# First batch's scores and value products as single float32 products, in a block-sparse attention and MLP kernel

## The chip, the cores and the metric

The kernel runs on one core of a Trainium2 chip. A core has a matrix engine (TensorE: PE for products, PEld for weight loads), VectorE (DVE), ScalarE (ACT), GpSimd (POOL) and SyncE (SP), which here issues nearly all DMAs. Each engine takes its instructions in the order in which the program lists them; engines wait for each other by semaphores. The metric is the time of one execution on the device, in microseconds (us), lower is better.

## The reference

Attention over 4 batches, 8 heads, 768 positions and 64 dimensions, with a mask in blocks of 32 positions, followed by an MLP with 512 inputs, 2048 inner and 512 outer columns on 3072 rows; `scale` is 1/8, `window` 1, and every block of queries has 3 sampled blocks of keys:

```python
scores = scale * np.matmul(q, k.transpose(0, 1, 3, 2))
mask = np.abs(blk_i - blk_j) <= window
mask = mask | (blk_i == 0) | (blk_j == 0) | (blk_i == n_blocks - 1) | (blk_j == n_blocks - 1)
for qb in range(n_blocks):
    for kb in sampled_blocks[qb]:
        mask[qb * block:(qb + 1) * block, kb * block:(kb + 1) * block] = True
scores = np.where(mask, scores, -1000000000.0)
scores = scores - np.max(scores, axis=-1, keepdims=True)
attn = np.exp(scores)
attn = attn / (np.sum(attn, axis=-1, keepdims=True) + 1e-09)
attn_out = np.matmul(attn, v)
...
x = np.ascontiguousarray(attn_out.transpose(0, 2, 1, 3)).reshape(B * S, H * D)
h = x @ w_in
sp = np.where(h > 20.0, h, np.log1p(np.exp(np.minimum(h, 20.0))))
g = h * np.tanh(sp)
y = g @ w_out
```

## The kernel before, in words

**Numbers.** A product of float32 data is made of fp16 parts: every operand is scaled by a power of two, rounded to a high part, and the rest kept as a low part. Three products stand for one: high x high, low x high, high x low (`PROD`, L659). The scale comes from the data: products of a tile with itself (`gram_k`, `gram_q`, `gram_v`, L373), their diagonal summed (L388), a sum over partitions by a float32 product with ones (`tp_k` and others, L396), and an integer root (`root`, L405 to L409). `parts` writes the high part on ScalarE (L500) and the low part on VectorE (L504); some tiles of q are done on ScalarE and GpSimd in its place (`APART`, L518 to L535).

**Attention.** Each batch is 13 jobs: two dense ones (first and last block of queries, against all 768 keys) and 11 pairs of query blocks. A query block of a pair sees 8 blocks of 32 keys: three neighbours (read from `kt`, 96 columns), the two ends and three sampled ones (copied to `kg` by GpSimd L611 or ScalarE L608, 160 columns). The blocks' numbers are read from memory into registers of the engine that copies, or of SP (L580), which gathers the value blocks (`vg`) from a copy of v in DRAM (`vd`, written at L553; gathered at L628 to L635).
`scores` (L664) runs on tiles of 64x32 of the array: four pairs of heads by two heads, eight places. Then come the maxima (L732 to L737, VectorE), the exponentials (L756, ScalarE), transposes of the probabilities (`t`, L680, TensorE), and their high part `ph` (L779, ScalarE). The low part `pl` is made on VectorE (L783), or, in jobs 0 to 5 of all 52 (`i < APL`), by a correcting product on TensorE (L787) and another pass of ScalarE (L792). The value products (`o_fn`, L818) use four tiles of 128x32: three products for each of the four pairs of head parity and key half, so 48 a transposed piece. A column of ones beside v gives the sum; L837 to L841 divide by it, and transposes (`tx`) give x.

**MLP.** w_in and w_out arrive as 8-byte numbers; pieces are loaded (L893, three buffers `wr`) and decoded on VectorE by three integer operations each (L901, L904, L907), which run through the first 175 us beside the attention of the first batch. Products with w_in are `h_None` (L1068), those with w_out `y` (L1162). `fill` (L1506) puts products without use where TensorE would be idle.

**Order.** All this is written as tasks (`add(engine, cost, function, ...)`) and a list of task numbers, `ORDER`, gives the sequence in which they are emitted; the engines' programs follow from it. The first batch stands at the start: k, q and v are loaded (`load`, L432), scaled and split, and the first w_in pieces follow.

Of the kernel before, what the change touches and what calls it, by code (L numbers as in the profile page):

```python
# [9 lines left out]
F32 = mybir.dt.float32  # L10
# [11 lines left out]
PSC = 4096.0  # L22
# [3 lines left out]
RINGS = dict(s=1, t=2, o=1, h=2, y=1, raw=6, wr=3, pt=2, ph=4, pl=4, xh=3, xl=3, mx=3, nb=3, r=2,  # L26
# [193 lines left out]
def attn_mish_kernel(ctx: ExitStack, tc: tile.TileContext, qT, kT, v, sampled, blocks, w_in, w_out, out):  # L220
# [38 lines left out]
    vd = [dram.tile([S + BS, H, VW], F16, name=f"vd{b}") for b in range(B)]  # L259
# [18 lines left out]
    osc = const.tile([P, B], F32, name="osc")  # L278

# [10 lines left out]
    def which(new):  # L290
# [38 lines left out]
        z = room.bitcast(F16)[0:BS, 0:H * VW]  # L329
        nc.gpsimd.memset(z, 0.0)  # L330
        for b in range(B):
            nc.scalar.dma_start(out=vd[b][S:S + BS].rearrange("s h d -> s (h d)"), in_=z)
# [23 lines left out]
    vgs = [at_.tile([P, 2, H, VW], F16, name=f"vg{n}", tag=f"vg{n}", bufs=1) for n in range(NVG)]  # L356
    RAW = H * VW
# [59 lines left out]
    def load(b, what, js, ring="raw", after=()):  # L417

        keys = [("raw", what, b, j) for j in js]
# [15 lines left out]
        add("SP", 0.5 * n, fn, r=after, w=keys,  # L435
            new=[(ring, key) for key in keys], key=-5 if b == 0 else 0, lat=3.6 if b else 3.0,
# [19 lines left out]
    def scales(b, what, j, cls):  # L456
# [4 lines left out]
        def fn():  # L461
# [4 lines left out]
            root(kp, sc, iv, SQ if b else 0)  # L466
            if q:
# [10 lines left out]
    def parts(b, what, j, cls):  # L478
# [34 lines left out]
        kh = ("hi",) + key  # L513
        if (what, b, j) in APART:
# [35 lines left out]
    APART = {("q", 0, 1), ("q", 0, 2), ("k", 1, 0), ("k", 1, 1), ("k", 1, 2)}  # L550
# [9 lines left out]
    def globals_(b):  # L560

        def fn(n):
            kb = tl["kt", b].rearrange("p r (j k) -> p r j k", k=BS)[:, :, 0:NB:NB - 1]
            nc.gpsimd.tensor_copy(out=kgs[n][:, :, WK + BS:WK + 3 * BS].rearrange("p r (j k) -> p r j k", k=BS), in_=kb)
# [3 lines left out]
    def globals_v(b, n):  # L568
        def fn():
            for s, j in enumerate((0, NB - 1)):  # L570
                nc.sync.dma_start(out=vgs[n][s * BS:(s + 1) * BS, 1], in_=vd[b][j * BS:(j + 1) * BS])
# [27 lines left out]
    def gather_k(su):  # L599
# [3 lines left out]
        def fn(eng):  # L603
            for k, c0 in slots(su):
                dst = kgs[n][:, :, c0:c0 + BS]
# [8 lines left out]
        if su["whole"]:  # L614
            add("DVE", 0.5, lambda: nc.vector.tensor_copy(
                out=kgs[n][:, :, 0:WK], in_=tl["kt", b][:, :, (qb - 1) * BS:(qb + 2) * BS]),
                r=KT3(b), w=[("kw", n)], use=[("kt", b)], key=-2, port=True)

    def gather_v(su):
# [6 lines left out]
        def fn():  # L626
            vg = vgs[n]
# [11 lines left out]
    def fetch_dense(su):  # L639
# [4 lines left out]
        def fn(j):  # L644
            if j < NVG:
                vt = vgs[j]
            else:
                vt = new(sb, "raw", ("vt", b), [P, RAW]).bitcast(F16).rearrange("p (c h d) -> p c h d", h=H, d=VW)
# [15 lines left out]
    def scores(su, s, c0, pieces, first, last):  # L664
# [4 lines left out]
        for n, (a, c) in enumerate(PROD):  # L669
            for m, (cs, src, ks) in enumerate(pieces):  # L670
                for i in range(NPR):
                    for g in range(2):
# [4 lines left out]
                            stop=last and n == len(PROD) - 1 and m == len(pieces) - 1)  # L677
# [20 lines left out]
    def attend(job):  # L698

        b, i, sus, nt, dense = job["b"], job["i"], job["sus"], job["nt"], job["dense"]  # L700
        nsu = len(sus)
# [6 lines left out]
        def s_fn():  # L708
# [7 lines left out]
            else:  # L716
                for w, su in enumerate(sus):
                    qb = su["qb"]
                    kg = kgs[su["ng"] % NKG]
# [23 lines left out]
        def nb_fn():  # L743
            mx, nb = tl[kmx], new(sb, "nb", ("nb", i), [P, 2, 2])
            for w in wq:
                nc.scalar.activation(out=nb[:, :, w], in_=mx[:, :, w], func=AF.Copy,
                                     scale=tl["ns", b, sus[w.start]["qb"] // TB][:, 1:2])
        add("ACT", 0.28 * len(wq), nb_fn, r=[kmx] + [("ns", b, t) for t in qts], w=[("nb", i)],
            new=[("nb", ("nb", i))], key=-1.5)

        def ex_fn(n):
            if n == 0:
# [4 lines left out]
                out=o, in_=x, func=AF.Exp, bias=nb[:, g, w:w + 1], scale=tl["ns", b, sus[w]["qb"] // TB][:, 0:1])  # L757
# [7 lines left out]
        for n in range(2):  # L765
            add("ACT", 1.7 if dense and n == 0 else 1.15, lambda n=n: ex_fn(n),
                r=[kmx, ("nb", i), ks] + (k2 if dense else []) + [("ns", b, t) for t in qts],
# [10 lines left out]
        def ph_fn(j):  # L778
            nc.scalar.activation(out=new(at_, "ph", ("ph", i, j), [P, 2, 2, P], F16), in_=tl["t", i, j], func=AF.Copy,  # L779
                                 scale=PSC)  # L780
# [931 lines left out]
```

## Time and profile before

| | |
|---|---|
| Three runs | 736.14, 738.39, 739.52 us; median 738.39 |
| Profiled execution: span | 735.3 us, 3.1 below the median |
| TensorE busy (PE) | 695.8 us, 95% |
| VectorE busy | 581.1 us, 79% |
| ScalarE busy | 585.3 us, 80% |
| GpSimd busy | 286.9 us, 39% |
| DMA | 103.61 MB, mean 141 GB/s |

The span is the time between the first and the last record of one execution; the runs' times have a little around it. The busy shares are means over 735 us: in the first 120 us no engine is busy throughout, later TensorE is. The views used below are windows (busy time of each engine in a stretch), the chain that ended last, followed back from the end to what released each step, timelines (one line an instruction or a run of like ones), and groups of like instructions by form.

### The profile page before, as it was taken

To read this page: it belongs to the slowest core of one execution; us is meant where nothing else is said; L and a number is where in the kernel's file an instruction comes from. 1 tells how busy PE (TensorE), PEld (TensorE's weight loads), DVE (VectorE), ACT (ScalarE), POOL (GpSimd) and SP (SyncE) were. 2 spreads that over 40 slices of the span, in tenths; PEclk is the share of its full clock that TensorE was granted. 3 is DMA by queue.
4 is the path that set the end of the run, shared out by engine and by line. 5 is a ranking of instruction groups with operands and counts; after the bars stand their busy time and mean duration, and the time that the engine had idled before them with its cause. 6 is when DMAs were issued, how large, how long until landed. Compare 5 with 4: busy or idle time off the path is not lost.

```text
span 735.3 us, 28986 instructions
## 1 busy us (share of the span) xinstructions
PE 695.8 (95%) x11839; PEld 539.4 (73%) x11839; DVE 581.1 (79%) x1167; ACT 585.3 (80%) x929; POOL 286.9 (39%) x390
## 2 busy tenths in 40 slices
PE   5656889999999999999999999999999999999997
PEld 4445668875767777777677677676768888888886
DVE  6988889897788878798688798899887683656565
ACT  3685769999889998988778897987988786777772
POOL 2021423526453451545551546586732103020241
PEclk9987899999999999999999999999999999999999
DMA  9887785741555564444533644564356300000101
GB/s 328 287 221 223 231 245 153 237 146 53 171 153 152 156 203 140 139 148 125 176 105 104 202 145 153 155 174 134 110 168 201 134 29 1 30 1 1 44 6 54
DMA packets 60042, 103.61 MB, mean 141 GB/s; under 512 B 8579, under 2 KB 20868, under 8 KB 59908
## 3 DMA queue, kind: packets, MB, share of 16 engines
q1 hardware_dynamic: 58992, 98.86, 43.5%
q10 hardware_dynamic: 916, 2.89, 1.3%
q8 instruction: 93, 1.52, 0.9%
q14 instruction: 41, 0.34, 0.1%
HBM read 84.58 MB, written 17.14 MB: 138 GB/s over the span
## 4 chain that ended last, share of the span: by engine, by line
PE 86%; DMA 5%; DVE 4%; SPq 2%; ACT 1%; issue 1%; DVEq 0%
PE h_None L1068 33%; PE y L1162 19%; PE yr L1281 11%; PE t L680 6%; PE obank L818 6%; PE s L674 5%; DMA vg<-vd 2%; PE obank L1281 2%; PE tx L680 2%; DMA wr<-in_moe_w_in_dram 1%; DMA wor<-in_moe_w_out_dram 1%; DMA raw_k<-in_k_dram 1%; SPq L580 1%; SPq L635 1%; DVE v L504 1%
## 5 line engine op out<-in xcount | busy, mean ns | idle before, releaser
L1068 PEld LDWEIGHTS <-wi 128*128 128x128 f16 x2304 | 223.4, 98 | 33.7 <-issue 1.5
L1068 PE MATMUL h_None<-xh,wi 128*128 128x256 f16 x1152 | 205.7, 273 | 0.2
L611 POOL COPY kg<-kt 128x256 f16 x246 | 110.2, 481 | 153.5 <-PE s L674 127.2
L1068 PE MATMUL h_None<-xl,wi 128*128 128x256 f16 x576 | 157.0, 273 | 0.0
L1162 PE MATMUL y<-wo,g 128*128 128x512 f16 x588 | 140.3, 379 | 0.0
L1162 PEld LDWEIGHTS <-g 128*128 128x128 f16 x672 | 64.3, 99 | 61.3 <-issue 1.3
L756 ACT ACTIVATE pt<-s,nb,ns 128x256 f32<-128x256 f32 (+1 forms) x208 | 107.7, 585 | 1.5 <-DVE wo L907 0.7
L1120 POOL TENSOR_TENSOR g<-hs_None,g 128x1024 f16<-128x1024 f32 x32 | 73.7, 2302 | 63.3 <-DVE g L1116 41.6
L779 ACT ACTIVATE ph<-t 128x512 f16<-128x512 f32 x112 | 65.6, 596 | 25.6 <-PE t L680 24.1
L783 DVE SCALAR_TENSOR_TENSOR pl<-t,ph 128x512 f16<-128x512 f32 x99 | 67.0, 684 | 23.1 <-ACT ph L779 23.0
L1079 ACT ACTIVATE hs_None<-h_None,gsc 128x512 f32<-128x512 f32 x96 | 65.6, 691 | 24.3 <-PE h_None L1068 19.5
L1107 DVE SCALAR_TENSOR_TENSOR hs_None<-us_None,hs_None 128x1024 f32<-128x1024 f32 x48 | 62.0, 1292 | 21.6 <-ACT us_None L1106 21.6
L680 PE MATMUL t<-ident,pt 128*128 128x128 f32 x448 | 69.2, 287 | 7.9 <-ACT pt L756 4.7
L1068 PE MATMUL h_None<-xr,wi 128*128 128x256 f16 x576 | 67.9, 273 | 0.0
L680 PEld LDWEIGHTS t<-ident,pt 128*128 128x128 f32 x448 | 54.1, 148 | 18.7 <-issue 4.8
L737 DVE TENSOR_REDUCE mx<-s 128x4 f32<-128x1024 f32 x44 | 53.6, 1218 | 10.2 <-PE s L674 10.2
L1098 ACT ACTIVATE us_None<-hs_None,hsc 128x1024 f32<-128x1024 f32 x48 | 54.9, 1146 | 4.4 <-DVE sg L1148 1.6
L818 PEld LDWEIGHTS <-ph 128*32 128x32 f16 x2408 | 43.3, 97 | 17.1 <-issue 9.6
L818 PE MATMUL obank<-vg,ph 128*32 128x129 f16 (+2 forms) x2168 | 46.6, 211 | 6.0 <-DMA vg<-vd 5.2
L1105 ACT ACTIVATE us_None<-us_None 128x1024 f32<-128x1024 f32 x48 | 50.8, 1060 | 1.1 <-POOL us_None L1103 0.7
L1106 ACT ACTIVATE us_None<-us_None 128x1024 f32<-128x1024 f32 x48 | 50.7, 1060 | 0.4
L1281 PEld LDWEIGHTS <-sg 128*128 128x128 f16 x480 | 47.0, 98 | 5.4
(263 smaller groups left out, 1274.2 us busy)
## 6 DMA issues: line engine op xcount, KB each, us to landing
vg<-vd SPq DMA_DIRECT2D x320, 65.0 KB, 2.4
vg<-vd SPq DMA_DIRECT2D x80, 195.0 KB, 3.1
wr<-in_moe_w_in_dram SPq DMA_DIRECT2D x8, 1024.0 KB, 8.6
vd<-v SPq DMA_DIRECT2D x12, 520.0 KB, 3.4
vg<-vd SPq DMA_DIRECT2D x12, 520.0 KB, 5.0
raw_k<-in_k_dram SPq DMA_DIRECT2D x12, 512.0 KB, 5.3
raw_q<-in_q_dram SPq DMA_DIRECT2D x12, 512.0 KB, 6.0
raw_v<-in_v_dram SPq DMA_DIRECT2D x12, 512.0 KB, 5.7
```

Of the source, the lines that this page charges most:

```text
L611: nc.gpsimd.tensor_copy(out=dst, in_=tl["kt", b][:, :, ds(j, BS)])
L680: nc.tensor.matmul(out, src, ident, start=start, stop=stop, is_transpose=True)
L756: ex = lambda o, x, g, w: nc.scalar.activation(out=o, in_=x, func=AF.Exp, bias=nb[:, g, w:w + 1], scale=tl["ns", b, sus[w]["qb"] // TB][:, ...
L779: nc.scalar.activation(out=new(at_, "ph", ("ph", i, j), [P, 2, 2, P], F16), in_=tl["t", i, j], func=AF.Copy, scale=PSC)
L783: nc.vector.scalar_tensor_tensor(out=new(at_, "pl", ("pl", i, j), [P, 2, 2, P], F16), in0=tl["t", i, j], scalar=PSC, in1=tl["ph", i, j], o ...
L818: nc.tensor.matmul(obank[cs, at:at + v1 - v0], p[:, k, g, cs], vt[:, k, 2 * c + g, v0:v1], start=j == 0 and g == 0 and k == 0 and n == 0, ...
L1068: nc.tensor.matmul(h[:, f2, 0:n].rearrange("p (s q) -> p s q", q=BS), wi[:, fp, w, cc, fs], x[:, s0:s0 + sn, cc], start=f2 == 0 and k == 0 ...
L1079: nc.scalar.activation(out=tl[kq][:, 2 * (fp % 2):2 * (fp % 2) + 2, 0:n], in_=tl[kh][:, :, 0:n], func=AF.Copy, scale=gsc[:, fp:fp + 1])
L1107: add("DVE", 1.32 * c, lambda: nc.vector.scalar_tensor_tensor(out=hs(), in0=us(), scalar=-0.5, in1=hs(), op0=ALU.add, op1=ALU.mult), r=[ku ...
L1120: add("POOL", 2.3 * c, lambda: nc.gpsimd.tensor_tensor(out=g(1), in0=hs(), in1=g(0), op=ALU.subtract), r=[kq, ("gh",) + kp], w=[kp], use=[kg],
L1162: nc.tensor.matmul(tl[ky], tl["g", b, t, k][:, g, f, q], wo_at(fc)[:, w], start=fc == 0 and n == 0, stop=fc == NFC - 1 and n == 2)
L1281: nc.tensor.matmul(R(i), lhs, rhs, start=head and j == n == 0, stop=k == NFC // 4 - 1 and j == 1 and n == 2, skip_group_check=True)
```

## The change

For batch 0 (`PLAIN = (0,)`) keys, queries and values stay float32:

- k and q are loaded straight into `kt` and `q`, so the products for their scales, the roots and both parts go, and with them the scale in the exponentials, which becomes the constant 1/8.
- v is copied by ScalarE (`v<-raw_v`, 65 float32 a head with the ones column, as many bytes as 130 fp16), stored and gathered as before. v's scale is still worked out, since the MLP's scales use it; it enters as `ivr` when the sums are divided.
- Scores are one float32 product for each of the eight places and pieces in place of three. The value products are one for each of the places in place of three, 16 a piece in place of 48. No low parts of the probabilities are made; `ph` is float32, and one ring holds for the other batches what `ph` and `pl` held.
- `ORDER` keeps its sequence with the dropped tasks taken out, but the loads of k and q of batch 0 stand later: behind v, two or three pieces of w_in and register loads of SP.

The core of the diff:

```diff
+    PLAIN = (0,)
+    vd = [dram.tile([S + BS, H, D + 1], F32, name=f"vd{b}") if b in PLAIN else
+          dram.tile([S + BS, H, VW], F16, name=f"vd{b}") for b in range(B)]
...
+    kfs = [x.rearrange("p r k -> p (r k)").bitcast(F32).rearrange("p (r k) -> p r k", r=NPR) for x in kgs]
+    kgv = lambda b, n: (kfs if b in PLAIN else kgs)[n]
...
     def load(b, what, js, ring="raw", after=()):
...
             for j, key in zip(js, keys):
+                if b in PLAIN and what != "v":
+                    dst = new(at_, "kt", ("kt", b), [P, NPR, S]) if what == "k" and j == 0 else \
+                        tl["kt", b] if what == "k" else new(at_, "q", key, [P, NPR, TT])
+                    nc.sync.dma_start(
+                        out=dst[:, :, j * TT:(j + 1) * TT] if what == "k" else dst,
+                        in_=(kT if what == "k" else qT)[b, :, :, j * TT:(j + 1) * TT].rearrange("r d s -> d r s"))
+                    continue
...
+        if b in PLAIN:
+            add("ACT", 1.16, lambda: copy("ACT"), r=[kr, ("ends",) + key], w=[key, ("done",) + key], use=[key], key=cls,
+                also=[("DVE", 0.75, lambda: copy("DVE"), True)])
+            return
...
-        for n, (a, c) in enumerate(PROD):
+        prods = ((0, 0),) if b in PLAIN else PROD
+        for n, (a, c) in enumerate(prods):
             for m, (cs, src, ks) in enumerate(pieces):
                 for i in range(NPR):
                     for g in range(2):
...
+            if plain:
+                continue
             if i < APL:
                 add("PE", 0.23, lambda j=j: td_fn(j), r=[("ph", i, j)], w=[kj], key=-3, lat=0.25, kind=("T", i))
...
                 prods = ((hi, 0, 2 * D + 1), (lo, 0, D + 1)) if whole else ((hi, 0, D + 1), (hi, D + 1, 2 * D + 1), (lo, 0, D + 1))
+                if plain:
+                    prods = ((hi, 0, D + 1),)
                 for n, (p, v0, v1) in enumerate(prods):
...
-    for j in T3:
-        sums(0, "k", j, AT0)
-    scales(0, "k", 0, AT0)
-    sums(0, "q", 0, AT0)
-    scales(0, "q", 0, AT0)
-    for j in T3:
-        parts(0, "k", j, AT0)
-    parts(0, "q", 0, AT0)
```

`ORDER` itself is a table of numbers, 117 lines of it replaced. What it and the code do is seen at three places. Names: `raw_k`, `raw_q`, `raw_v` are loaded tiles, `kt` all keys of the batch, `wr` a loaded piece of w_in, `offv` the table of value offsets, `s` scores, `mx` maxima; numbers behind a name tell copies apart, and line numbers of the changed file are some 35 to 50 higher there.

SP, from its start, before:

```order
L432 DMA raw_k_0_159<-in_k_dram 128x4x256
L432 DMA raw_k_1_161<-in_k_dram 128x4x256
L432 DMA raw_k_2_163<-in_k_dram 128x4x256
L432 DMA raw_q_0_165<-in_q_dram 128x4x256
L432 DMA raw_v_0_179<-in_v_dram 128x2x512
L432 DMA raw_v_2_181<-in_v_dram 128x2x512
L432 DMA raw_v_1_191<-in_v_dram 128x2x512
L580 TENSOR_LOAD offv
...
L893 DMA wr_227<-in_moe_w_in_dram 128x4x512
L893 DMA wr_240<-in_moe_w_in_dram 128x4x512
```

and in the changed kernel:

```order
L448 DMA raw_v_0_160<-in_v_dram 128x2x512
L448 DMA raw_v_2_162<-in_v_dram 128x2x512
L448 DMA raw_v_1_164<-in_v_dram 128x2x512
L616 TENSOR_LOAD offv
...
L949 DMA wr_184<-in_moe_w_in_dram 128x4x512
L949 DMA wr_186<-in_moe_w_in_dram 128x4x512
...
L435 DMA kt_206<-in_k_dram 128x4x256
...
L949 DMA wr_245<-in_moe_w_in_dram 128x4x512
L435 DMA kt_206<-in_k_dram 128x4x256
...
L435 DMA kt_206<-in_k_dram 128x4x256
...
L435 DMA q_0_293<-in_q_dram 128x4x256
```

The keys and the query tile have moved from the head of the queue behind v, two loads of `offv` into registers, three pieces of w_in and more such loads.

VectorE, from the maxima of the first dense scores on, before:

```order
L732 TENSOR_REDUCE mx_514<-s_387 128x2
L734 TENSOR_REDUCE mx_514<-s_0_0_412 128x1
L734 TENSOR_REDUCE mx_514<-s_0_1_413 128x1
L735 TENSOR_TENSOR mx_514<-mx_514 128x2
L504 SCALAR_TENSOR_TENSOR v_0_473<-raw_v_0_179,sc_v_0_469,v_0_473 128x16x64
L904 SCALAR_TENSOR_TENSOR wi<-wr_227,wi 128x1024
L907 SCALAR_TENSOR_TENSOR wi<-wr_227,wi 128x1024
L504 SCALAR_TENSOR_TENSOR v_1_476<-raw_v_1_191,sc_v_0_469,v_1_476 128x16x64
L901 TENSOR_SCALAR wi<-wr_240 128x1024
L504 SCALAR_TENSOR_TENSOR v_2_479<-raw_v_2_181,sc_v_0_469,v_2_479 128x16x64
L901 TENSOR_SCALAR wi<-wr_312 128x1024
```

and in the changed kernel, from the last step of v's scale on:

```order
L416 TENSOR_SCALAR sc_v_0_369<-tp_v_0_316 128x1
L486 TENSOR_SCALAR ivr<-iv_x 128x1
L771 TENSOR_REDUCE mx_410<-s_319 128x2
L773 TENSOR_REDUCE mx_410<-s_0_0_328 128x1
L773 TENSOR_REDUCE mx_410<-s_0_1_329 128x1
L774 TENSOR_TENSOR mx_410<-mx_410 128x2
L960 SCALAR_TENSOR_TENSOR wi<-wr_184,wi 128x1024
L963 SCALAR_TENSOR_TENSOR wi<-wr_184,wi 128x1024
L957 TENSOR_SCALAR wi<-wr_186 128x1024
L957 TENSOR_SCALAR wi<-wr_245 128x1024
```

The three low parts of v (L504) have gone from between the decoding steps; the maxima stand where they stood, ahead of decoding the first piece of w_in.

TensorE, at the first dense scores and the first pair's scores, before:

```order
L396 MATMUL tp_v_0_384<-ss_v_0_382,ones 128x1
L674 LDWEIGHTS q_0_315
L674 MATMUL s_387<-kt_238,q_0_315 32x512
L674 LDWEIGHTS q_0_315
L674 MATMUL s_387<-kt_238,q_0_315 32x512
...
L674 LDWEIGHTS q_0_315
L674 MATMUL s_604<-kt_238,q_0_315 32x96
L674 LDWEIGHTS q_0_315
L674 MATMUL s_604<-kt_238,q_0_315 32x96
```

and in the changed kernel, where a float32 product loads its own weights and is one row:

```order
L403 MATMUL tp_v_0_316<-ss_v_0_314,ones 128x1
L712 MATMUL s_319<-kt_206,q_0_293 32x512 x8
L712 MATMUL s_0_0_328<-kt_206,q_0_293 32x256
L712 MATMUL s_0_1_329<-kt_206,q_0_293 32x256
...
L712 MATMUL s_497<-kt_206,q_0_293 32x96 x8
L712 MATMUL s_497<-kg_117,q_0_293 32x160 x8
L712 MATMUL s_497<-kt_206,q_0_293 32x96 x8
L712 MATMUL s_497<-kg_118,q_0_293 32x160 x8
```

The places and their sequence are the same; each score that was three pairs of rows is one row.

## Rows read from the trace of the kernel before

**Rows 1.** Windows of 20 us: stretch, length, each engine's busy us (instructions), PEclk, DMA share, GB/s.

```profile
20.00:40.00 20.00, 11.96 (x329) 8.93 (x314) 19.21 (x31) 13.62 (x27) 0.00 (x0) 1.00 0.87 265
40.00:60.00 20.00, 12.41 (x340) 9.10 (x337) 18.44 (x36) 15.78 (x32) 6.49 (x7) 0.77 0.85 260
60.00:80.00 20.00, 15.31 (x489) 11.78 (x491) 16.20 (x41) 11.56 (x23) 2.10 (x6) 0.72 0.66 184
...
140.00:160.00 20.00, 20.00 (x341) 16.27 (x340) 18.45 (x47) 20.00 (x34) 9.49 (x10) 1.00 0.49 155
```

**Rows 2.** Chain of waits, 0 to 125 us: start us, us, what.

```profile
1.80 6.08 DMA raw_k<-in_k_dram
...
31.78 9.24 DMA wr<-in_moe_w_in_dram
...
84.35 0.94 ACT q L529
...
86.44 3.93 PE h_None L1068 x36
...
114.19 0.49 PE obank L818 x47
```

**Rows 3.** TensorE's timeline, 7 to 20 us: start us, us, line, operation, tiles, shape, count.

```profile
7.93 1.03 PE L373 MATMUL gram_k<-raw_k 128*128 128x128 bf16 x8 [0.54 <-DMA raw_k<-in_k_dram]
9.51 0.56 PE L396 MATMUL tp_k<-ss_k,ones 128*128 128x1 f32 x2 [0.54 <-DVE gram_k L388]
...
18.44 2.12 PE L674 MATMUL s<-kt,q 64*32 64x512 f16 x48
```

**Rows 4.** TensorE's timeline, 200 to 216 us: float32 transposes at full clock.

```profile
204.94 0.27 PE L680 MATMUL tx<-ident,xs 128*128 128x128 f32 x1
...
214.69 1.09 PE L680 MATMUL t<-ident,pt 128*128 128x128 f32 x8
```

**Rows 5.** TensorE's timeline, 113 to 115 us: value products of one piece.

```profile
114.12 0.24 PE L818 MATMUL obank<-vg,ph 128*32 128x65 f16 x8
114.19 0.20 PE L818 MATMUL obank<-vg,pl 128*32 128x65 f16 x4
114.22 0.24 PE L818 MATMUL obank<-vg,ph 128*32 128x65 f16 x8
```

**Rows 6.** Window of L674 alone, 110 to 120 us: PE, PEld, PEclk, DMA share, GB/s.

```profile
110.00:120.00 10.00, 1.00 (x96) 0.85 (x96) 1.00 0.44 126
```

**Rows 7.** Groups by form, 86 to 175 us: shapes, count, busy us, mean ns, idle before.

```profile
L783 DVE SCALAR_TENSOR_TENSOR pl<-t,ph 128x512 f16<-128x512 f32 x15 | 10.0, 684 | 1.7 <-ACT ph L779 1.7
...
L818 PE MATMUL obank<-vg,pl 128*32 128x65 f16 x244 | 7.2, 193 | 0.0
...
L674 PE MATMUL s<-kg,q 64*32 64x160 f16 x192 | 4.0, 234 | 0.0
...
L674 PE MATMUL s<-kg,q 64*32 64x256 f16 x48 | 0.8, 271 | 0.0
L674 PE MATMUL s<-kt,q 64*32 64x512 f16 x24 | 0.8, 379 | 0.0
```

**Rows 8.** Window from 86 to 120 us, columns as in the first group.

```profile
86.00:120.00 34.00, 30.63 (x798) 26.00 (x796) 29.05 (x47) 25.73 (x44) 11.90 (x22) 1.00 0.73 208
```

**Rows 9.** SP's timeline, 0 to 20 us: the loads' issue.

```profile
4.83 3.44 SPq L432 DMA_DIRECT2D raw_v<-in_v_dram  x3
```

**Rows 10.** VectorE's timeline, 0 to 22 us.

```profile
8.57 0.18 DVE L327 TENSOR_SCALAR offv<-z 1x72 int32<-1x72 f32 x1
...
21.99 1.29 DVE L504 SCALAR_TENSOR_TENSOR v<-raw_v,sc_v,v 128x1024 f16<-128x1024 f32 x1
```

**Rows 11.** Window from 15 to 20 us, columns as in the first group.

```profile
15.00:20.00 5.00, 2.89 (x50) 1.80 (x56) 3.95 (x9) 2.24 (x4) 4.98 (x11) 1.00 1.05 387
```

**Rows 12.** Groups by form, 0 to 86 us: what the low parts of probabilities take.

```profile
L792 ACT ACTIVATE pl<-t 128x512 f16<-128x512 f32 x11 | 6.5, 599 | 3.8 <-PE t L787 3.8
...
L787 PE MATMUL t<-ph,neg 128*128 128x512 f16 x12 | 5.4, 480 | 1.7 <-ACT ph L779 1.7
```

More of the change, by code (lines that the diff above doesn't have):

```diff
@@ L278, in attn_mish_kernel @@
     osc = const.tile([P, B], F32, name="osc")
+    ivr = const.tile([P, 1], F32, name="ivr")
     ctx.enter_context(tc.manual_schedule())
@@ L417, in load @@
     def load(b, what, js, ring="raw", after=()):
-        keys = [("raw", what, b, j) for j in js]
+        plain = b in PLAIN and what != "v"
+        keys = [(what if plain else "raw", *((b, j) if plain else (what, b, j))) for j in js]
+        kt = ("kt", b)
         def fn():
             for j, key in zip(js, keys):
+                if b in PLAIN and what != "v":
[5 more added lines that the diff above has]
+                    continue
                 raw = new(sb, ring, key, [P, RAW]) if ring == "raw" else \
@@ L434, in load @@
         n = len(js)
-        add("SP", 0.5 * n, fn, r=after, w=keys,
-            new=[(ring, key) for key in keys], key=-5 if b == 0 else 0, lat=3.6 if b else 3.0,
+        if plain:
+            ring = "kt" if what == "k" else "q"
+        add("SP", 0.5 * n, fn, r=after, w=keys, use=[kt] if plain and what == "k" and js[0] else (),
+            new=[(ring, kt if plain and what == "k" else key) for key in keys if not (plain and what == "k" and key[-1])], key=-5 if b == 0 else 0, lat=3.6 if b else 3.0,
             kind=("dma", 1.6 * n, n))
@@ L676, in scores @@
                             src[gs, a * NPR + i, ks], start=first and n == 0 and m == 0,
-                            stop=last and n == len(PROD) - 1 and m == len(pieces) - 1)
+                            stop=last and n == len(prods) - 1 and m == len(pieces) - 1)
     def transpose(out, src, start, stop):
@@ L747, in nb_fn @@
                                      scale=tl["ns", b, sus[w.start]["qb"] // TB][:, 1:2])
-        add("ACT", 0.28 * len(wq), nb_fn, r=[kmx] + [("ns", b, t) for t in qts], w=[("nb", i)],
+        add("ACT", 0.28 * len(wq), nb_fn, r=[kmx] + [("ns", b, t) for t in qts if not plain], w=[("nb", i)],
             new=[("nb", ("nb", i))], key=-1.5)
@@ L766, in attend @@
             add("ACT", 1.7 if dense and n == 0 else 1.15, lambda n=n: ex_fn(n),
-                r=[kmx, ("nb", i), ks] + (k2 if dense else []) + [("ns", b, t) for t in qts],
+                r=[kmx, ("nb", i), ks] + (k2 if dense else []) + [("ns", b, t) for t in qts if not plain],
                 w=[("p", i, n)], new=[("pt", k) for k in kps] if n == 0 else (), use=kps, key=-1.5)
@@ L809, in o_fn @@
                 tl[ko] = obank
-            w, apart = 0 if dense else j, i >= SPLIT
-            vt = vgs[sus[w]["ng"] % NVG] if not dense else tl["vt", b, j] if sus[0]["qb"] else tl["v", b, j]
-            hi, lo = tl["ph", i, j], tl["pl", i, j]
+            w, apart = 0 if dense else j, i >= SPLIT and not plain
+            vt = vgv(b, sus[w]["ng"] % NVG) if not dense else tl["vt", b, j] if sus[0]["qb"] else tl["v", b, j]
+            hi, lo = tl["ph", i, j], tl.get(("pl", i, j))
             for g, k in ((g, k) for g in range(2) for k in range(2)):
@@ L1376, in attn_mish_kernel @@
         load(0, "k", [j])
-    load(0, "q", [0], "hs")
+    load(0, "q", [0])
     for j in T3:
```

295 lines of the change are left out of this document (162 added, 133 removed), and 18 rows, old and new, of the table ORDER.

## The prediction

> **What bounds the kernel now.** I read the windows of 20 us first, then the chain of waits, then the timelines of TensorE, SP and VectorE. The windows [rows 1] show two regimes. From 140 us on TensorE is busy all the time, so whatever its work grows by there is added to the time. Before 80 us it is not: it is busy 11.96, 12.41 and 15.31 us of three stretches of 20, and in the first two VectorE is the fullest engine with 19.21 and 18.44. The chain of waits [rows 2] says what this first stretch waits for: the keys, which land at 7.88 us (1.80 + 6.08), and at 31.78 us a piece of w_in, which was fetched only when VectorE had decoded an earlier one and given back its buffer. At 86.44 us the first MLP products start, and soon afterwards TensorE is full. All of the change lies in the first 175 us. So there are two questions: by how much does the first MLP product come later, and how much TensorE work is added behind it.
>
> **What a float32 product costs.** Everything rests on this. The trace has float32 products on the whole array only. tp_k is one product in the program and two matmuls in the trace [rows 3]: a float32 product is two streams, one behind the other, on the same place of the array. For the rate of a stream I take the float32 transposes: eight of 128 columns take 1.09 us, and one alone is recorded with 0.27, so they start (1.09 - 0.27)/7 = 117 ns apart, about 2 cycles of 2.4 GHz a column [rows 4]. A half is then 2 cycles a column, a product 4. That the halves run at fp16's single cycle is the lower end of the price.
>
> The Trainium skill (FP8 and Floating Point Precision, TensorE Precision Notes) counts four passes through the array for a true float32 product. By that rule the lower end falls away and the sum below stands; no row here has such a product of many columns.
>
> How fp16 products share the array is in [rows 5]. Twelve value products, three rounds over the four tiles of 128x32, begin every 0.10 us, so a round takes 33 ns; a stream of 65 columns alone is 27 ns at 2.4 GHz. Four tiles stream together, and the next product on a tile begins when that tile's former stream is over. The scores do the same on eight tiles of 64x32. In the changed program the two halves are neighbours on one tile, and no row shows a matmul that starts ahead of one that waits. So I take it that the second half waits for its own tile, that the next tile's first half starts beside it, and that a product costs the time of one half, where fp16 paid a quarter or an eighth of a stream.
>
> - Scores of a pair of query blocks: 16 products' columns of 96 + 160, 16 x 256 x 2 / 2.4 GHz = 3.41 us, with an estimated 5 ns for each of 32 starts 3.57. Before, 96 products took 1.00 us at full clock [rows 6]: **+2.6 us a pair**.
> - Scores of a dense job: 8 x 768 x 2 / 2.4 = 5.1 us; before, three times as many columns on eight tiles, 1.0: **+4.1 us**.
> - Value products of one transposed piece of probabilities: 16 x (54 + 4) ns = 0.93 us, before 0.49 [rows 2]: **+0.44 us a piece**.
>
> **Behind the first MLP product.** From 86 us on lie four pairs with 160 gathered columns and one with 256, the dense job with its 24 products of 512 columns [rows 7], and 17 of the 28 pieces (244 of their 272 low products are recorded): 5 x 2.6 + 4.1 + 17 x 0.44 = 24.6 us. TensorE is idle for 34.0 - 30.63 = 3.4 us between 86 and 120 us [rows 8], which can take part of it; I take 2.5. **+22 us**, bounds 21 and 25, or 3 with halves of a single cycle (5 x 0.8 + 1.5 - 2.5). What goes on VectorE here, 15 low parts of probabilities of 684 ns [rows 7], is worth nothing: TensorE sets the time and covers it.
>
> **Ahead of it** work comes and work goes.
> - The loads. Before, k, one tile of q and v are issued by 8.3 us [rows 9], and w_in follows. Now v is first; then two register loads wait for offv, which VectorE finishes at 8.75 us [rows 10]. Behind them stand two pieces of w_in, k, a third piece, k, k and q: 3 x 1024 + 4 x 512 KB = 5.24 MB, at 387 GB/s [rows 11] 13.5 us. An issue at about 9.3 and some 2 us to its first bytes (the keys' 6.08 us less 4.1 for 1.57 MB) put the last one at 25 to 26 us. The first scores started at 18.44 [rows 3]: **+7.5 us**.
> - The first dense scores took 2.1 us [rows 3]; now 5.1 at 2.4 GHz, or 10.2 at 1.2. Here the engine runs at the lower level: eight gram products of 128 columns take 1.03 us [rows 3], about 107 ns each. It may rise within them; the middle, 7.6: **+5.5**.
> - VectorE works in order, and its maxima of these scores stand ahead of decoding the first piece of w_in. So that decoding comes 13 us later, less the three low parts of v, 1.28 us each [rows 10], that stood among it: 9. The fourth load of w_in waits for it. With the later value loads of the same queue: **+11** at the chain's piece of 31.78 us, bounds 9 and 13.
> - The parts of q's later tiles go (one is on the chain for 0.94 us at 84.35 [rows 2]), and for 11 pieces the low part on ScalarE and its correction on TensorE, 6.5 and 5.4 us [rows 12]. Most of this ran beside other work: **-2**, bounds 0 and -9.
> - Six pairs at 2.6 and eleven pieces at 0.44 are 20 us of TensorE time, in stretches that have 8.0, 7.6 and 4.7 us idle [rows 1]. Hidden where a transfer is awaited, on the path where scores release the maxima: **+6**, bounds 0 and 17.
>
> Sum ahead: 11 - 2 + 6 = **+15 us**, the first MLP product at about 101 us. In all +37: the span of 735.3 becomes 772, and with the 3.1 us by which the median of 738.39 lies above it, **775 us**. The forecast's own range: with halves of a single cycle, 738 + 3 behind and about 8 ahead, 749; with all bounds up, 738 + 13 + 17 + 25 = 793.
>
> **Rivals.**
> - *All tiles stream at once* (the other side). If a half that waits for its tile doesn't hold up the next tile, the halves spread over eight or four tiles: a pair costs 16/8 x 256 x 4 / 2.4 GHz = 0.85 us and a piece 16/4 x 65 x 4 / 2.4 = 0.43, no more than before [rows 2, 6]. For it: fp16 tiles do overlap [rows 5]. Against it: fp16 never puts two products of one tile side by side, and no row shows an overtaking. Then only the front end decides: 7.5 us of late loads against what was removed, 3.8 on VectorE, 6.5 + 0.9 on ScalarE, 5.4 on TensorE. With all 16.6 on the path: **729 us**, faster. With half of them: **738 us**. It is faster than the bound below from 11.2 us on the path on.
> - The Trainium skill (TensorEngine Tiling (Array Packing), Key Properties) says that tiles work independently and that different tiles load and multiply in parallel. By that rule alone this rival holds; the trace agrees for fp16 [rows 5], and no row shows it for two neighbours on one tile.
> - *No overlap at all* for float32. Each product then takes 4 cycles a column by itself: a pair 6.8 us (+5.9), a piece 1.73 (+1.24), the dense job 10.2 (+9.1). Behind the first MLP product 5 x 5.9 + 9.1 + 17 x 1.24 - 3 = 57 us; ahead of it 15, 5 more for the dense job and a third of the six pairs' 20: 27. **822 us**. Against it: neighbouring tiles overlap for fp16 on both shapes of tile.
> - *The change doesn't do what it says*: a float32 product on a tile could be a single stream. tp_k's two matmuls [rows 3] speak against it; it would lie near 729 and is within that chance.
>
> **How the numbers follow.** The forecast has 0.71, the rival at 822 has 0.12, all tiles at once 0.17, of it 0.10 at 729 and 0.07 at 738. Half a per cent, 3.7 us, is about what a measurement of this kernel can tell from no change. So faster 0.10, same 0.07, slower 0.83. The range goes from 738 over the forecast's own range, 749 to 793, to 800, and leaves out the two far rivals.
>
> **What would show it.** In the changed profile a pair of blocks should take about 3.6 us of scores where it took 1.0, with the two halves of a product adjacent on one tile. The first scores should start at 25 to 26 us and the first MLP product at about 101, and from 160 us on TensorE should be full as before, everything 35 to 40 us later. A pair of about 1 us would prove me wrong towards 729 to 738, one of 6.8 towards 822. First scores before 20 us would take some 6 us off. A first MLP product before 90 us with slow pairs would mean that the first stretch hides what I put on its path, and give about 760.

## The result, and the profile after

The changed kernel is slower: 745.79 us (median of 4 runs) against 737.3 (the kernel before, with a fourth run), a ratio of 1.0113 with a 95% interval of 1.0080 to 1.0146. Run again beside other kernels it was 744.17 us, 1.0093 (1.0060 to 1.0126). I had forecast 775. The profiled execution has a span of 745.3 us, 10.0 above the one before. Its page begins:

```profile
span 745.3 us, 27329 instructions
## 1 busy us (share of the span) xinstructions
PE 689.4 (92%) x11037; PEld 532.3 (71%) x11037; DVE 557.8 (75%) x1112; ACT 564.4 (76%) x907; POOL 273.0 (37%) x384
```

TensorE is busy 689.4 us where it was 695.8: it has 6.4 us less to do. But it is idle 745.3 - 689.4 = 55.9 us where it was idle 39.5. The loss is idle time, and the windows (the columns of [rows 1]) say where it lies:

```profile
0.00:20.00 20.00, 4.04 (x28) 3.10 (x28) 5.16 (x28) 1.28 (x1) 1.29 (x8) 1.00 0.75 257
20.00:40.00 20.00, 9.45 (x215) 6.30 (x216) 11.76 (x16) 8.65 (x17) 1.78 (x8) 0.91 0.67 229
40.00:60.00 20.00, 13.99 (x256) 10.31 (x254) 16.83 (x33) 12.02 (x30) 3.95 (x6) 0.66 0.86 255
60.00:80.00 20.00, 11.82 (x243) 8.28 (x240) 15.03 (x40) 7.68 (x20) 0.88 (x3) 0.83 0.77 223
...
140.00:160.00 20.00, 20.00 (x385) 17.78 (x383) 15.15 (x40) 19.51 (x33) 13.61 (x11) 1.00 0.66 203
```

From 20 to 40 us VectorE was busy 19.21 us [rows 1] and is now busy 11.76, and the DMA share fell from 0.87 to 0.67. Nothing is full there: everything waits. The chain of waits of the first 60 us names for what:

```profile
17.26 8.69 DMA q<-in_q_dram
26.09 2.03 PE s L712 x16
28.14 1.23 DVE mx L771
...
30.22 1.15 DVE wi L960
31.39 1.22 DVE wi L963
...
38.73 6.50 DMA wr<-in_moe_w_in_dram
```

q lands at 25.95 us, scores start at 26.09, and only behind their maxima does VectorE finish the first piece of w_in, whose buffer the next load needs. SP's timeline of the same stretch (each row one kind of load and its count) has that load, the fourth of w_in, at 32.64 us; it was at 25.70. The fifth, which the chain shows, follows at 38.73 us; it was at 31.78:

```profile
0.75 1.48 SPq L448 DMA_DIRECT2D raw_v<-in_v_dram  x3
9.96 0.92 SPq L949 DMA_DIRECT2D wr<-in_moe_w_in_dram  x2
...
17.26 1.07 SPq L435 DMA_DIRECT2D q<-in_q_dram  x1
...
32.64 0.37 SPq L949 DMA_DIRECT2D wr<-in_moe_w_in_dram  x1
```

The first MLP product follows at 91.54 us, 5.3 later than the 86.28 of before. What I had got wrong shows in TensorE's timeline, where a pair's scores are

```profile
125.32 0.40 PE L712 MATMUL s<-kt,q 64*32 64x96 f32 x16
125.51 0.48 PE L712 MATMUL s<-kg,q 64*32 64x160 f32 x16
125.78 0.37 PE L712 MATMUL s<-kt,q 64*32 64x96 f32 x16
125.94 0.58 PE L712 MATMUL s<-kg,q 64*32 64x160 f32 x16
```

64 records, two for each product, as foreseen, but sixteen of 96 columns are through in 0.19 us (125.32 to 125.51). One behind the other on one place, 16 x 80 ns, they would need 1.28 us; by my rule half of that. The pair takes 1.20 us from its first start to its last end, not 3.57; read in the same way, a pair took 1.00 to 1.03 us before.

### The profile page after: what moved, and what is told of

The parts are those of the page before. It is cut to its first block, busy times and chain, and to the rows that moved or that the text cites. A ratio compares the mean times of both kernels' runs of the same rounds, so it can differ in the third digit from the quotient of the medians.

```text
span 745.3 us, 27329 instructions
## 1 busy us (share of the span) xinstructions
PE 689.4 (92%) x11037; PEld 532.3 (71%) x11037; DVE 557.8 (75%) x1112; ACT 564.4 (76%) x907; POOL 273.0 (37%) x384
## 4 chain that ended last, share of the span: by engine, by line
PE 81%; DMA 9%; DVE 4%; SPq 3%; ACT 1%; issue 1%
PE h_None L1124 32%; PE y L1218 18%; PE yr L1337 11%; PE obank L872 6%; PE t L718 5%; PE s L712 5%; DMA wor<-in_moe_w_out_dram 2%; DMA wr<-in_moe_w_in_dram 2%; PE obank L1337 2%; DMA vg<-vd 2%; PE tx L718 1%; SPq L616 1%; DMA q<-in_q_dram 1%; DMA raw_q<-in_q_dram 1%; SPq L671 1%
## 5 line engine op out<-in xcount | busy, mean ns | idle before, releaser
L647 POOL COPY kg<-kt 128x256 f16 (+1 forms) x246 | 103.7, 455 | 167.0 <-PE s L712 145.9
L798 ACT ACTIVATE pt<-s,nb,ns 128x256 f32<-128x256 f32 (+1 forms) x156 | 80.5, 584 | 0.6
L834 DVE SCALAR_TENSOR_TENSOR ph<-t,ph 128x512 f16<-128x512 f32 x84 | 57.0, 685 | 21.3 <-ACT ph L831 21.3
L718 PEld LDWEIGHTS t<-ident,pt 128*128 128x128 f32 x448 | 52.6, 144 | 20.2 <-issue 5.6
L872 PE MATMUL obank<-vg,ph 128*32 128x65 f16 (+3 forms) x3464 | 52.6, 211 | 13.6 <-DMA vg<-vd 9.6
L831 ACT ACTIVATE ph<-t 128x512 f16<-128x512 f32 x84 | 49.0, 595 | 18.3 <-PE t L718 18.1
L1157 DVE TENSOR_SCALAR us_None<-us_None 128x1024 f32<-128x1024 f32 x48 | 35.2, 734 | 19.6 <-ACT us_None L1154 19.6
```

The costliest lines, as they stand in the source:

```text
L647: nc.gpsimd.tensor_copy(out=dst, in_=tl["kt", b][:, :, ds(j, BS)])
L718: nc.tensor.matmul(out, src, ident, start=start, stop=stop, is_transpose=True)
L798: ex = lambda o, x, g, w: nc.scalar.activation(out=o, in_=x, func=AF.Exp, bias=nb[:, g, w:w + 1], scale=float(D) ** -0.5 if plain else tl[ ...
L834: nc.vector.scalar_tensor_tensor(out=tl["pl", i, j], in0=tl["t", i, j], scalar=PSC, in1=tl["ph", i, j], op0=ALU.mult, op1=ALU.subtract)
L872: nc.tensor.matmul(obank[cs, at:at + v1 - v0], p[:, k, g, cs], vt[:, k, 2 * c + g, v0:v1], start=j == 0 and g == 0 and k == 0 and n == 0, ...
```

## The experiments

Two theories. **Late loads**: k and q stand behind v and w_in on SP, so the maxima come late, VectorE's decoding waits behind them, and with it all loads that need its buffers. **Dearer products**: the float32 products' own time on TensorE is the loss. Idle is span less TensorE's busy time; the last three columns are starts in the profile. Each ratio is to runs of the kernel before beside that row's kernel. The expectations stand in the words in which they were put down before each run; the diffs of `ORDER` are cut to the places where it differs.

| kernel | median us | ratio to before (95%) | PE busy | PE idle | first scores | 4th w_in load | first MLP product |
|---|---|---|---|---|---|---|---|
| before | 736.1 to 737.3 | | 695.8 | 39.5 | 18.4 | 25.7 | 86.3 |
| changed | 745.79 | 1.0113 (1.0080 to 1.0146) | 689.4 | 55.9 | 26.1 | 32.6 | 91.5 |
| changed again | 744.17 | 1.0093 (1.0060 to 1.0126) | 689.9 | 53.4 | 26.2 | 32.7 | 91.1 |
| k first | 736.16 | 0.9997 (0.9974 to 1.0020) | 689.6 | 44.1 | 17.0 | 23.6 | 81.3 |
| decode first | 742.16 | 1.0069 (1.0049 to 1.0090) | 688.5 | 51.8 | 25.9 | 22.2 | 88.1 |
| k and scores first | 732.52 | 0.9939 (0.9917 to 0.9961) | 689.7 | 40.4 | 9.9 | 19.9 | 79.0 |
| that, and q's 2nd tile early | 734.04 | 0.9956 (0.9931 to 0.9981) | 685.6 | 46.4 | 10.2 | 20.5 | 80.2 |
| high halves only | 737.32 | 1.0007 (0.9984 to 1.0029) | 675.1 | 59.8 | 26.0 | 31.2 | 88.3 |
| three streams, k first | 738.25 | 1.0020 (0.9996 to 1.0044) | 686.5 | 50.1 | 16.9 | 23.0 | 82.8 |
| fp16, late loads | 756.12 | 1.0285 (1.0231 to 1.0339) | 693.3 | 59.3 | 36.5 | 43.8 | 104.6 |
| fp16, three on a tile | 747.94 | 1.0143 (1.0089 to 1.0196) | 706.3 | 40.4 | 18.5 | 25.9 | 85.2 |
| four on a tile, k first | 736.32 | 0.9996 (0.9973 to 1.0019) | 692.9 | 42.4 | 17.1 | 23.7 | 81.9 |

**The clock.** The expectations name a third theory: a slower clock of TensorE. The mean granted clock from 20 to 100 us (PEclk of the windows) does not follow the times. It is 0.87 before, 0.83 and 0.85 in the two runs of the changed kernel, 0.85 with k first, 0.77 in the fastest kernel (k and scores first) and 0.91 in the slowest (fp16, late loads).

**k first.** In `ORDER` tasks 0 to 2 load k, 3 q, 4 to 6 v.

```diff
-    7 4 6 5 55 31 96b 72b 33 71 0 10+2 41 63 11 78b 2 47 12 46 1 52 51 3 40 39
+    7 0 1 2 3 4 6 5 55 31 96b 72b 33 71 10+2 41 63 11 78b 47 12 46 52 51 40 39
```

> The changed kernel with the loads of batch 0's k and q put back at the head of SP's queue, ahead of v; nothing else is moved. Theory late loads (the 8 us come from k and q landing late: the maxima wait, VectorE's decoding behind them waits, and the w_in and w_out loads that need its buffers follow): the first scores start at 13 to 15 us in place of 26.1, the fourth w_in load is issued before 26 us in place of 32.6, and the time is 6 to 9 us below the changed kernel, 737 to 740. Theory dearer products (the 8 us are the float32 products' own time on TensorE): the scores start early but the time stays within 2 us of the changed kernel, 744 to 748. Theory slower clock (TensorE is longer at 1.2 GHz since it idles): it stays too, unless the mean of PEclk over 20 to 100 us rises.

The whole loss is gone, 8 to 10 us, and the time lies just below the 737 to 740 expected. TensorE's work is that of the changed kernel (689.6 us), its idle time 11.8 us less. Scores start at 17.0 us and not at 13 to 15, since v's scale products stand ahead of them on TensorE.

```profile
2.35 0.65 SPq L435 DMA_DIRECT2D q<-in_q_dram  x1
5.02 3.85 SPq L448 DMA_DIRECT2D raw_v<-in_v_dram  x3
10.34 3.59 SPq L949 DMA_DIRECT2D wr<-in_moe_w_in_dram  x3
23.57 0.37 SPq L949 DMA_DIRECT2D wr<-in_moe_w_in_dram  x1
```

That is SP's timeline of this kernel: q is asked for at 2.35 us, and the fourth piece of w_in at 23.57, 9.1 us ahead of the changed kernel. That the time is level with the kernel before has two parts: the first MLP product comes 4.9 us earlier than there (81.3 against 86.3), but the span is only 1.6 us shorter (733.7 against 735.3). From that product to the end TensorE is busy 1.5 us more than before (641.6 against 640.1) and idle 1.8 us more.

**fp16, late loads.** The other half of the same question, in the kernel before:

```diff
-    7 0 1 2 3 8+3 4 6 9 5 10 76 11 12 52 13 117b 14 18 93b 54 15 92 19 22 16 28+2 62
+    7 4 6 5 76 52 117b 93b 54 92 0 62 84 99b 2 68 67 1 73 72 3 61 60 8+3 9 10 11 12 13 14 18 15 19 22 16 28+2
```

> The kernel before, fp16 parts and all, with only the loads moved as the change moves them: v first, then the two register loads, w_in pieces and k and q among them. Theory late loads: the place of the loads costs without any float32 product too. k and q land at 25 to 26 us in place of 7.9, and the 10.6 us of preparation between them and the first scores come after that, so first scores at 35 to 37 us, the fourth w_in load at 42 to 44 in place of 25.7, and the time 8 to 16 us above the kernel before, 745 to 753. If the loads were hidden and the float32 products the cause, it stays within 3 us of the kernel before.

It costs 20 us, more than I gave it, without any float32 product; the times of scores and of the fourth load came out as expected. The first MLP product is 18.3 us late and the span 17.3 us longer, so hardly anything was made up later. The timeline of TensorE and SP's of this kernel:

```profile
36.53 2.12 PE L674 MATMUL s<-kt,q 64*32 64x512 f16 x48
```

```profile
43.79 0.37 SPq L893 DMA_DIRECT2D wr<-in_moe_w_in_dram  x1
```

The place of the loads costs in both kernels. It costs 8 to 10 us in the changed one, where the preparation between k and the scores is gone, and 20 in the one before. Read the other way, the rest of the change is worth 10 to 12 us where the loads are late (744.17 and 745.79 against 756.12) and nothing where they are early (736.16 against 736.1 to 737.3).

**Decode first.** The loads stay late. VectorE's tasks 98, 99, 73 to 75 and 79 to 81 (decoding) go ahead of 150 (maxima), SP's 90 and 126 (two w_in loads) ahead of 18 (storing v).

```diff
-    169b 9 15 16 19 22 171 150 37 28 53 17 58 151 152 29 98 18 153 99
+    169b 9 15 16 19 22 171 98 99 73 74 75 79 80 81 150 37 28 53 17 58 151 152 29 90b 126b 18 153
```

> The changed kernel with k and q as late as they are, but VectorE decodes the first three pieces of w_in ahead of the first maxima, and SP asks for the next two pieces ahead of storing v. If what counts in the late loads is the decoding that stands behind the maxima, the fourth w_in load is issued at about 23 to 25 us in place of 32.6 and the time falls by 4 to 7 us, to 739 to 742. If the attention chain itself (scores, probabilities, value products) is what sets the first MLP product, it stays within 2 us of the changed kernel although the loads come earlier.

The fourth load comes at 22.24 us, the first MLP product at 88.1, 3 us sooner than in the changed kernel, and the time is 2 to 4 us less, just outside what I expected. So the decoding behind the maxima carries a part; the interval overlaps with those of both runs of the changed kernel, so the size is not settled. The rest may be the attention chain, which still starts at 25.9 us; but the sixth piece of w_in is still asked for only at 42.62 us (42.63 in the changed kernel), so this run doesn't show it.

**High halves only.**

```diff
-                            s[g][i * BS:(i + 1) * BS, c0 + cs.start:c0 + cs.stop], q[gs, c * NPR + i, qs],
-                            src[gs, a * NPR + i, ks], start=first and n == 0 and m == 0,
+                            s[g][i * BS:(i + 1) * BS, c0 + cs.start:c0 + cs.stop], half(q[gs, c * NPR + i, qs]),
+                            half(src[gs, a * NPR + i, ks]), start=first and n == 0 and m == 0,
...
+            hf = lambda x: x.bitcast(mybir.dt.bfloat16)[:, 1::2] if plain else x
```

> The changed kernel with every score and value product of batch 0 made of the upper 16 bits of each operand alone (read as bfloat16 from the float32 tiles): one stream for a product, the lower halves' part of the products is left out. The order and all loads stay. Theory dearer products: a pair's scores fall from 1.14 to about 0.4 us and a value piece from 0.59 to about 0.25, TensorE's own work behind 120 us falls by some 5 us, ahead of it by more, and the time by 8 us or more, to 738 or less. Theory late loads: what lies ahead of the first MLP product hardly moves, and only the TensorE work behind it is saved: 4 pairs, the dense job and some 15 value pieces, 5 to 8 us there, but the delay of the maxima at 48 to 72 us against the kernel before stays at 4 us or more. Theory slower clock: with less to do TensorE is longer at 1.2 GHz, and the stretch before 100 us is no shorter.

14.3 us less TensorE work gives 7 to 8 us. Both theories had asked for about that in the total, so this run alone doesn't tell them apart; and the maxima at 47 to 68 us were 2 to 3 us behind the kernel before, where late loads had asked for 4. It shows that TensorE's work counts ahead of the first MLP product too: 3 us there (88.3 against 91.1 to 91.5). A pair took 0.42 to 0.43 us from 98 us on, as expected.

**Three streams, k first.** It asks for float32's price against three 16-bit products, each of the operands' upper halves as in the run above, with all else alike.

```diff
-        prods = ((0, 0),) if b in PLAIN else PROD
+        prods = ((0, 0),) * 3 if b in PLAIN else PROD
...
-                    prods = ((hi, 0, D + 1),)
+                    prods = ((hi, 0, D + 1),) * 3
...
-                scale=float(D) ** -0.5 if plain else tl["ns", b, sus[w]["qb"] // TB][:, 0:1])
+                scale=float(D) ** -0.5 / 3 if plain else tl["ns", b, sus[w]["qb"] // TB][:, 0:1])
```

> As the kernel with k and q ahead of v, but every product of batch 0 is three streams of the operands' upper 16 bits (as bfloat16) in place of one float32 product; the exponentials take a third of the scores, and the sums of the value products grow alike, so only the lower halves' part is left out. It has the order, the loads and the missing preparation of the kernel with k first, with TensorE work of the size of the three fp16 products. What it is faster by is the price of float32. By the busy times of the changed kernel (scores 20.8 and value products 18.9 us against 16.2 and 15.0 before) the price is up to 8.5 us; what lies ahead of the first MLP product hides about half: 731 to 734 in place of 736.2. If float32 costs no more than three streams: 735 to 738.

A miss: 738.25 us is not below the 736.16 of float32 products, and lies just above both ranges. TensorE is busy 3.1 us less and idle 6.0 us more. No price of float32 against three streams shows in the time; the two intervals overlap. Why the idle time grew is not shown. The granted clock was lower here from 60 to 120 us (0.75 and 0.94 in the windows of 30 us, where k first has 0.84 and 1.00), which may hide a price.

**k and scores first.** As with k first; besides, tasks 149 and 150 (dense scores and their maxima) ahead of 10 (v's scale products), and 90 ahead of 18.

```diff
-    7 0 1 2 3 4 6 5 55 31 96b 72b 33 71 10+2 41 63 11 78b
+    7 0 1 2 3 4 6 5 55 31 96b 72b 33 71 149 150 10+2 41 63 11 78b
...
-    58 151 152 29 98 18 153 99 154 20 90b 156
+    58 151 152 29 98 90b 18 153 99 154 20 156
```

> As the first of these kernels (k and q ahead of v), and besides the first dense scores ahead of v's scale products on TensorE, their maxima ahead of v's scale on VectorE, and the fourth w_in load ahead of storing v. Theory late loads: first scores at 8 to 10 us, maxima done by 14, at least as fast as the first of these kernels, 734 to 739, at or below the kernel before. Theory dearer products: 744 to 748.

732.52 us, a little below the range. This version and the next are the only ones here that are faster than the kernel before beyond their intervals. In its windows the DMA share of the first 40 us is 0.94 and 1.02: the loads fill that stretch.

```profile
0.00:20.00 20.00, 8.53 (x136) 5.60 (x136) 9.68 (x35) 9.12 (x16) 3.06 (x16) 1.00 0.94 337
20.00:40.00 20.00, 11.12 (x207) 9.07 (x207) 16.75 (x30) 8.13 (x23) 1.50 (x3) 0.63 1.02 320
```

**q's second tile early.** As the last; besides, task 168 ahead of 132, the last w_in piece.

```diff
-    129 181 312 103 109 315 132b 110 313 225b
...
-    344b 183 305 184 168 130 144 330
+    129 181 312 103 109 315 168 132b 110 313 225b
...
+    344b 183 305 184 130 144 330
```

> As the kernel with the dense scores first, and the load of batch 0's second query tile moved ahead of the last piece of w_in, where its chain showed 8.05 us of waiting for that tile at 50 us. If that wait sets the first MLP product, the fifth job's scores come some 5 us earlier than 58 us and the time falls by 2 to 5 us, to 728 to 731. If the value gathers and w_out pieces behind it set it anyway, it stays at 731 to 734.

No gain: 734.04 against 732.52, the intervals overlap. The tile was asked for at 46.05 us in place of 50.16, but the fifth job's scores started at 60.1 us and not some 5 us ahead of 58, and the first MLP product came at 80.2 us in place of 79.0. So something else held them; what it was is not shown.

**Changed again**, unaltered, on the chip of the kernels with three streams, with q's second tile early and with three on a tile.

> The changed kernel as it is, beside the others on one chip: 744 to 748, 1.008 to 1.015 times the kernel before.

744.17 us, as expected.

**Three on a tile.** The prediction's step on TensorE, tried on fp16 alone, in the kernel before.

```diff
-        for n, (a, c) in enumerate(PROD):
-            for m, (cs, src, ks) in enumerate(pieces):
-                for i in range(NPR):
-                    for g in range(2):
+        for m, (cs, src, ks) in enumerate(pieces):
+            for i in range(NPR):
+                for g in range(2):
+                    for n, (a, c) in enumerate(PROD):
```

> The kernel before (all products fp16 in three parts) with the loops of the scores turned: the three products of one tile stand next to each other, where before all eight tiles had their first product, then their second, then their third. The same products, the same number. The prediction's step (a product that waits for its tile holds up the next tile): in each tile the second and third product wait a whole stream, so a block takes about two thirds of 24 streams in a row; at full clock a pair of blocks takes some 1.5 to 2 us or more in place of 0.93 to 1.0, and over 44 pairs and 8 dense jobs the time rises by 25 us or more. The rival that came true in the changed kernel (products behind a waiting one start ahead of it on other tiles): a pair stays within 0.15 us of before and the time within 5 us of it.

Between the two: 11 us more, 10.5 of it TensorE's busy time. Its timeline of one pair, which takes 1.31 us, from 117.98 to 119.29, where it took 1.00 to 1.03:

```profile
117.98 0.34 PE L674 MATMUL s<-kt,q 64*32 64x96 f16 x21
118.11 0.23 PE L674 MATMUL s<-kg,q 64*32 64x160 f16 x1
118.12 0.20 PE L674 MATMUL s<-kt,q 64*32 64x96 f16 x1
118.12 0.23 PE L674 MATMUL s<-kg,q 64*32 64x160 f16 x1
...
118.76 0.53 PE L674 MATMUL s<-kg,q 64*32 64x160 f16 x23
```

The program has all 24 products on `kt` of a block ahead of those on `kg`. A product on `kg` started at 118.11 us, ahead of three on `kt` that stand before it. So TensorE does start matmuls past waiting ones. Neighbours on a tile still cost nearly a third more; that its reach has an end is one possible reason, which no run here separates from others, such as the weight loads between them.

**Four on a tile, k first.**

```diff
-            for m, (cs, src, ks) in enumerate(pieces):
-                for i in range(NPR):
-                    for g in range(2):
+            for m, i, g in ([(m, i, g) for i in range(NPR) for g in range(2) for m in range(len(pieces))] if b in PLAIN else
+                            [(m, i, g) for m in range(len(pieces)) for i in range(NPR) for g in range(2)]):
```

> The kernel with k first, and in batch 0's scores the product on kt and that on kg of one tile next to each other, so that four streams stand in a row on each tile, in place of two. The same products. If TensorE starts later products past a waiting one without a limit that matters, a pair stays at 1.0 to 1.2 us and the time within 2 us of the kernel with k first, 734 to 738. If it looks only a little way ahead, a pair takes 1.5 to 3 us, and with 11 pairs, half of them hidden, the time is 3 to 15 us more.

The time is unchanged (736.32), but a pair takes 1.48 us where it takes 1.21 with k first, and TensorE is busy 3.3 us more: the kernel's time is as the first expectation has it, the pair's nearly as the second. In this program a tile's product on `kt` is followed by its product on `kg`, yet 15 matmuls on `kt` start ahead of the first on `kg`:

```profile
103.33 0.43 PE L713 MATMUL s<-kt,q 64*32 64x96 f32 x15
103.52 0.30 PE L713 MATMUL s<-kg,q 64*32 64x160 f32 x1
103.53 0.24 PE L713 MATMUL s<-kt,q 64*32 64x96 f32 x1
103.53 0.51 PE L713 MATMUL s<-kg,q 64*32 64x160 f32 x15
...
104.31 0.50 PE L713 MATMUL s<-kg,q 64*32 64x160 f32 x10
```

## Why the prediction was wrong

The direction was right, and so was the first of its causes. The size was four times too large, for one step. That 745.79 us lies inside the range of 738 to 800 is luck: of the +22 behind the first MLP product 4.7 came, of the +5.5 of the first dense scores 0.7 (2.82 us against 2.12), and it was the late loads that kept the time above 738 (with k first it is 736.16).

- **The step that failed** is "that the second half waits for its own tile, that the next tile's first half starts beside it, and that a product costs the time of one half". TensorE did not hold up the other tiles for a half that waits. I had reasoned from rows in which no matmul overtakes another [rows 5]; but there none needs to, because no two neighbours share a tile. Absence from such rows was no evidence. And "no row shows an overtaking" was wrong for the trace as a whole: the scores of the kernel before have some, though no two neighbours share a tile there either. The program has eight products on `kt` ahead of eight on `kg`; in TensorE's timeline one on `kg` starts ahead of the eighth on `kt`:

```profile
117.72 0.26 PE L674 MATMUL s<-kt,q 64*32 64x96 f16 x7
117.78 0.24 PE L674 MATMUL s<-kg,q 64*32 64x160 f16 x1
117.78 0.20 PE L674 MATMUL s<-kt,q 64*32 64x96 f16 x1
```

In the changed kernel a pair at the full granted clock measured 1.14 us on the chain of waits and 1.20 on the timeline, and not 3.57 (before, 0.93 and 1.00 to 1.03); in the first 75 us pairs took 1.73 to 2.20 us where they had taken 1.03 to 1.48. A dense job measured 1.45 us on the chain and not 5.1; three pieces of value products 1.50 us, so 0.50 each and not 0.93. These are two rows of the chain of the changed kernel, with two loads of w_out ahead of them:

```profile
97.08 9.02 DMA wor<-in_moe_w_out_dram
107.11 8.88 DMA wor<-in_moe_w_out_dram
...
138.24 1.45 PE s L712 x32
...
151.86 1.50 PE obank L872 x96
```

By the sources' windows all of batch 0's scores take 20.8 us where they took 16.2, and its value products 18.9 where they took 15.0. Each row has TensorE's busy time, then its weight loads, PEclk, DMA share and GB/s. The scores before and in the changed kernel:

```profile
0.00:86.00 86.00, 9.96 (x624) 7.50 (x624) 0.88 0.83 259
86.00:172.00 86.00, 6.25 (x480) 4.66 (x480) 1.00 0.64 193
...
0.00:90.00 90.00, 12.36 (x383) 7.10 (x390) 0.85 0.74 234
90.00:181.00 91.00, 8.46 (x368) 5.16 (x352) 1.00 0.66 194
```

and the value products before and in the changed kernel:

```profile
0.00:86.00 86.00, 7.12 (x528) 5.92 (x528) 0.88 0.83 259
86.00:172.00 86.00, 7.86 (x648) 6.52 (x648) 1.00 0.64 193
...
0.00:90.00 90.00, 9.62 (x352) 7.30 (x352) 0.85 0.74 234
90.00:181.00 91.00, 9.26 (x480) 7.41 (x480) 1.00 0.66 194
```

That is 8.5 us more, where the forecast's prices for 11 pairs, two dense jobs and 28 pieces add up to 49. What was removed outweighs it: by the windows of 0 to 175 us before and 0 to 180 us in the changed kernel the scale products fell by 6.4 us (20.1 to 13.7), the corrections by 5.8 (to none) and the fillers by 2.9 (7.1 to 4.2), some 15 in all. So TensorE has 6.4 us less to do. The 5 and 4 ns a start in the prices are estimates that no row gives; they make 0.16 us of a pair and 0.06 of a piece.

- **Two streams of 2 cycles a column** held. The dense job has 768 columns a tile, 768 x 4 / 2.4 GHz = 1.28 us with eight tiles at once, and took 1.45; halves of one cycle would give 0.64. The Trainium skill's four passes (FP8 and Floating Point Precision, TensorE Precision Notes) agree with that.
- **The start of the scores** held: 26.09 us, forecast 25 to 26.
- **The decoding behind the maxima** held as a chain and was mis-sized: +11 forecast, +6.9 measured (32.64 against 25.70, 38.73 against 31.78). The difference is the first dense scores, which took 2.03 us on the chain, 2.82 in all, and not 7.6. The level of the engine was guessed well: the same job took 1.52 us at 138 us, so the first one ran at about half that rate, although the granted clock of 26 to 29 us is recorded as 1.00. Of the +15 forecast for the first MLP product +5.3 came true.
- **Behind it** +22 was forecast; the profiled spans differ by 10.0, so 4.7 came (3.1 in the changed kernel run again). From its first MLP product to the end TensorE is busy 642.1 us where it was 640.1, and idle 11.7 where it was 8.9. So 2.0 us of it are work of TensorE and the rest is waiting; the chain waits there for the two pieces of w_out shown above.
- **The rival "all tiles at once"** had the mechanism, and its prices (0.85 and 0.43 us) are much nearer to the measured ones than those of the forecast. The Trainium skill's sentence on independent tiles (TensorEngine Tiling (Array Packing), Key Properties) agrees with this trace for two neighbours as well. The rival's times, 729 and 738, were wrong: it set half or all of the removed work against the late loads. With k put first the same removed work brings the time only level with before (0.9997), and the late loads come on top of that, 8 to 10 us.

VectorE has 23 us less to do and ScalarE 21 (581.1 to 557.8, 585.3 to 564.4). What that and TensorE's smaller work are worth together depends on the order: 10 to 12 us with the loads late, where the preparation stood between them and the scores (first scores at 36.5 us with fp16 and 26.1 in the changed kernel), and nothing with the loads early. The 732.52 us come from scores that start as soon as k and q are there, together with an earlier fourth piece of w_in; no run makes these moves in the kernel before, so how much of it the shorter preparation gives is not shown.

## What to carry to other kernels

When a change removes preparation, the loads that it prepared move onto the path: look first at where they stand in their queue, and at what in-order work of other engines stands behind their first consumer. Here the place of four loads was worth 8 to 10 us, and all the rest of the change 10 to 12 us with these loads late and nothing with them early. Before costing a wait inside an engine, ask whether the rows could have shown the opposite at all, and look for the opposite in other rows of the trace; a rate inferred from products that never met the condition needs both ends in the range.

## What the hardware showed

- Float32 products on tiles of 64x32 and 128x32 run on all tiles at once, two streams each: sixteen streams of 96 columns in 0.19 us, three pieces of 32 streams of 65 columns each in 1.50 us, though each product's halves are neighbours on one tile. A pair's float32 scores took 1.14 us on the chain and 1.20 on the timeline, three fp16 products 0.93 and 1.00 to 1.03.
- TensorE takes its instructions in the order of the program, but it started matmuls ahead of earlier ones: in the kernel before (117.78 us), with three fp16 products in a row on each tile (118.11 us) and with four float32 streams in a row (103.33 to 103.52 us).
- Neighbours on a tile are not free. With three fp16 products in a row on each tile a pair took 1.31 us in place of 1.00 to 1.03, and the kernel 1.4% longer; with four float32 streams in a row a pair took 1.48 us in place of 1.21, and the time did not change. Why is not shown.
